# Chunk attention and two feed-forward layers on one core: another way to the transposes of q, k and the softmax weights

## The chip, the cores and the metric

The kernel runs on one core of one Trainium2 chip. The metric is the device time of one execution in microseconds; the median of the runs counts. Engines: TensorE (PE, with its weight loads as PEld), VectorE (DVE), ScalarE (ACT), GpSimd (POOL), and SyncE (SP), whose queue issues all DMAs here.

## The reference

Attention within chunks of 64 tokens, then two feed-forward layers on 4608 tokens of 512 features:

```python
scores = scale * matmul(q_c, k_c.T)              # q, k, v: (8, 8, 576, 64), chunks of 64
attn = exp(scores - max(scores))
attn = attn / (sum(attn) + 1e-09)
out = matmul(attn, v_c)                          # (8, 8, 576, 64)
x = out.transpose(0, 2, 1, 3).reshape(4608, 512)
h = x @ w_in;  g = h * sigmoid(1.702 * h);  x = g @ w_out                        # 512 -> 2048 -> 512
h = x @ w_in2; g = max(h, 0) + alpha * min(h, 0); out = g @ w_out2
```

## The kernel before, in words

Tokens are handled in 36 groups of 128 (two chunks of 64) and in blocks of 512 (four groups). Blocks 0 to 6 pass through the first layer in the plain way, one after another; each has 16 steps n (`NF`), one for each 128 of the 2048 hidden features. A step issues twelve matmuls into `psH` (`emit_h`, L599), a sigmoid-gelu and an fp32r cast of it on ACT (L609, L612), the subtraction that gives the low part on DVE (`gs`, L617), and, up to two steps later, twelve matmuls into `psY` (`emit_y`, L629). At a block's last step two y steps are issued, at its first one, at its second none. The last step of a block also splits the next block's x into high and low parts (`split_x`, L573 and L575, on ACT and DVE, once the block's last h matmuls are done), and after the last y step, in the next block's first step, four copies `ysb` (two on ACT, two on DVE, L642 and L644) are stored by four DMAs (L645). The second layer follows and is not touched by the change.

The attention of later groups is woven into these steps. `between` maps a half-slot (two for each step: one in the middle of `emit_h`, before `gs`; one after `emit_y`) to functions that are called there. A group has a base half-slot; from the fifth group in `GROUP_ORDER` on, bases are six half-slots apart (`PERIOD`), so a group's position relative to a block's start takes one of three values. Before the change a group g of the ninth and later (28 of them) goes like this:

- 24 to 20 half-slots before its base, `sort_qk` copies quarters of q and k from DRAM to a DRAM scratch tensor by eight strided DMAs (16 if the group straddles two batches); `load_sorted` (12 before) loads them sorted by two DMAs.
- `att_T` (6 before): two DVE transposes in 32x32 blocks (L402) give q and k with features on the partitions.
- The matmuls of S (`att_S_matmuls`, L449) are issued with `att_PV` of the group before, two half-slots before the base; `att_S_max` (1 before) takes the maximum and subtracts it on DVE (L460, L462); `att_X` is the exponential on ACT (L469, with an activation table load ahead of it and another ahead of the next gelu).
- `att_N` (at the base): sum, reciprocal, product on DVE (L474 to L477). `att_AT` (1 after): eight DVE transposes of 32 partitions each (L509), which put each 32x32 quadrant where it belongs. `att_PV` (4 after): 32 matmuls of 64x64 (L542), and then ACT copies to x.

Beside that, the second layer's weights are prepared every six half-slots: loads (`raw`, L242), decoding on DVE (L180 to L196), splits (`sta`, `stb`: a cast on ACT, a subtraction on POOL, L276) and stores two half-slots later (`send_due`, L253). Each engine and SP's queue take their instructions strictly in the order in which they are written.

Of the kernel before, what the change touches and what calls it, by code (L numbers as in the profile page):

```python
# [9 lines left out]
F32 = mybir.dt.float32  # L10
# [5 lines left out]
ALU = mybir.AluOpType  # L16
AX = mybir.AxisListType
# [47 lines left out]
def tile_chunk_attention_two_ffn(  # L65
# [269 lines left out]
    def load_qkv(g, names="qkv"):  # L335

        for nm in names:
            if g < GPB:
                t = {
                    "q": lambda: spare(f"wi{NF - GPB + g}", 0),  # L340
                    "k": lambda: spare(f"wi{NF - GPB + g}", 1),
                    "v": lambda: spare(f"wo{NF - 1 - g // 2}", g % 2),
                }[nm]()
            else:
                t = qkv_p.tile([P, 512], F32, tag=nm, name=nm, bufs=1 if nm == "v" else 2)
# [8 lines left out]
    def load_v(g):  # L354
        load_qkv(g, "v")

    qk_d = {}
    QK_AT = {GPB + 2: 3, GPB + 3: 9}

    def sort_qk(part, g):  # L360


        nm, src = (("q", q), ("k", k))[part // 4]
        if part % 4 == 0:
            qk_d[g, nm] = dram.tile([4, P, HP, SQ], F32, name=f"{nm}d_{g}")
        par, y = divmod(part % 4, 2)
        for off, n, b, s in spans(g * P, P):
            nc.sync.dma_start(
                out=qk_d[g, nm][part % 4, off:off + n],
                in_=src[b, par::2, s:s + n, y * SQ:(y + 1) * SQ].rearrange("h t e -> t h e"),  # L370
            )

    def load_sorted(g):
        for nm in ("q", "k"):
            t = qkv_p.tile([P, 512], F32, tag=nm, name=nm, bufs=2)
            nc.sync.dma_start(
                out=t, in_=qk_d.pop((g, nm)).rearrange("r (t b) h e -> (r t) (b h e)", b=4)
            )
            qkv[g, nm] = t

    qkT = {}

    def att_T(g):

        copies = []
        for nm in ("q", "k"):
            a = qkv.pop((g, nm))
            if g < GPB:
                t = spare(f"wo{NF - 3 - g % 2}", nm == "k").rearrange("p (h t) -> p h t", h=HP)
            else:  # L390
                t = qkt_p.tile([P, HP, P], F32, tag=nm + "T", name=nm + "T")
            if g < 2 * GPB:
                ps = psum_att("psT")
                for hp in range(HP):
                    nc.tensor.transpose(
                        ps[:, hp * P:(hp + 1) * P],
                        a[:, 2 * hp:2 * hp + 2, :].rearrange("p h d -> p (h d)"),
                        ident,
                    )
                copies.append((t.rearrange("p h t -> p (h t)"), ps))  # L400
            else:
                nc.vector.transpose(  # L402
                    t.rearrange("p h (t b) -> p b h t", b=4),
                    a.rearrange("p (b h e) -> p b h e", b=4, h=HP),
                )
            qkT[g, nm] = t
        for copy in copies:
            nc.scalar.copy(*copy)  # L408
# [31 lines left out]

    def att_S_matmuls(g):

        qt, kt = qkT.pop((g, "q")), qkT.pop((g, "k"))
        s_t[g] = s4 = both[0][:, :, HP * CH:].rearrange("p j (h t) -> p h j t", h=HP)
        for hp in range(HP):
            for c in range(2):
                for j in range(2):
                    r = slice(j * CH, (j + 1) * CH)
                    nc.tensor.matmul(  # L449
                        s4[c * CH:(c + 1) * CH, hp, j, :],  # L450
                        qt[r, hp, c * CH:(c + 1) * CH],
                        kt[r, hp, c * CH:(c + 1) * CH],
                        start=True,
                        stop=True,
                    )

    def att_S_max(g):
        s4 = s_t.pop(g)
        m = st_p.tile([P, HP, 2, 1], F32, tag="m", name="m")
        nc.vector.reduce_max(m, s4, axis=AX.X)  # L460
        e = e_p.tile([P, 2 * HP, CH], F32, tag="e", name="e")
        nc.vector.tensor_tensor(  # L462
            out=e.rearrange("p (h j) t -> p h j t", j=2), in0=s4,
            in1=m.to_broadcast([P, HP, 2, CH]), op=ALU.subtract,
        )
        e_t[g] = e

    def att_X(g):
# [1 line left out]

    def att_N(g):
        e = e_t[g]
        d = st_p.tile([P, 2 * HP, 1], F32, tag="d", name="d")
        nc.vector.reduce_sum(d, e, axis=AX.X)  # L474
        nc.vector.tensor_scalar_add(d, d, 1e-9)
        nc.vector.reciprocal(d, d)
        (nc.gpsimd if g < GPB - 1 or g in GROUP_ORDER[:GPB] else nc.vector).tensor_tensor(  # L477
            out=e, in0=e, in1=d.to_broadcast([P, 2 * HP, CH]), op=ALU.mult
        )

    def att_E(g):
        att_X(g)
        att_N(g)

    at_t = {}

    def att_AT(g):
        e = e_t.pop(g)
        if g < GPB:
            t = spare(f"wi{NF - GPB - 1 - g}", 1).rearrange("p (h t) -> p h t", h=HP)  # L490
        else:
            t = at_p.tile([P, HP, P], F32, tag="at", name="at")

        if g >= GPB:
            if g < 2 * GPB:
                ps = psum_att("psAT")
                for u in range(2 * HP):
                    for c in range(2):
                        r = slice(c * CH, (c + 1) * CH)
                        nc.tensor.matmul(  # L500
                            ps[r, u * CH:(u + 1) * CH], e[r, u, :], ident[r, r], start=True, stop=True
                        )
                nc.scalar.copy(t.rearrange("p h t -> p (h t)"), ps)
            else:
                t3 = t.rearrange("p h (j t) -> p (h j) t", j=2)
                for i in range(P // SQ):
                    for b in range(CH // SQ):
                        o = i // 2 * 2 + b
                        nc.vector.transpose(  # L509
                            t3[o * SQ:(o + 1) * SQ, :, i % 2 * SQ:(i % 2 + 1) * SQ],  # L510
                            e[i * SQ:(i + 1) * SQ, :, b * SQ:(b + 1) * SQ],
                        )
# [13 lines left out]
    def att_PV(g):  # L526
# [12 lines left out]
        for hp in range(HP):  # L539
            for c in range(2):  # L540
                for j in range(2):
                    nc.tensor.matmul(  # L542
                        ps[c][j * CH:(j + 1) * CH, hp * CH:(hp + 1) * CH],
                        vt[c * CH:(c + 1) * CH, 2 * hp + j, :],
                        at[c * CH:(c + 1) * CH, hp, j * CH:(j + 1) * CH],
                        start=True,
                        stop=True,
                    )
# [553 lines left out]
    with tc.manual_schedule():  # L1102
# [68 lines left out]
        def base(i):  # L1171
            return FIRST_BASES[i] if i < GPB else 8 * GPB + PERIOD * (i - GPB)
# [3 lines left out]
        for i, g in enumerate(GROUP_ORDER):  # L1176
            if i < GPB:
                times = ((att_T, -5), (att_X, -1), (att_N, 0), (att_AT, 3), (att_PV, 4))
            else:
                times = (  # L1180
                    (att_T, -6 if i > GPB else -8), (att_S_max, -1), (att_X, -1), (att_N, 0), (att_AT, 1), (att_PV, 4),
                )
            for fn, at in times:
                if g > GPB or fn is not att_T:
# [124 lines left out]
```

## Time and profile before

| | |
|---|---|
| median of 3 runs | 1554.39 us (1553.26 to 1555.19) |
| profiled execution, first to last instruction (span) | 1552.8 us; the profile gives no other time of its own, and the median lies 1.6 us above it |
| busy: PE, DVE, ACT, POOL | 1538.1, 1234.8, 894.1, 607.6 us |
| instructions | 25251 |
| DMA packets | 470282, of which 252688 under 512 B; 316.26 MB |

The page shows engines by busy time, the span in 40 slices, the DMA queues, the chain of work that ended last, and the costliest groups of instructions. A timeline row gives the start, the length and the engine of one or more like instructions; brackets at its end give the engine's idle time ahead of it and what ended that.

### The profile page before, as it was taken

To read this page: it belongs to the slowest core of one execution; us is meant where nothing else is said; L and a number is where in the kernel's file an instruction comes from. 1 tells how busy PE (TensorE), PEld (TensorE's weight loads), DVE (VectorE), ACT (ScalarE), POOL (GpSimd) and SP (SyncE) were. 2 spreads that over 40 slices of the span, in tenths; PEclk is the share of its full clock that TensorE was granted. 3 is DMA by queue.
4 is the path that set the end of the run, shared out by engine and by line. 5 is a ranking of instruction groups with operands and counts; after the bars stand their busy time and mean duration, and the time that the engine had idled before them with its cause. 6 is when DMAs were issued, how large, how long until landed. Compare 5 with 4: busy or idle time off the path is not lost.

```text
span 1552.8 us, 25251 instructions
## 1 busy us (share of the span) xinstructions
PE 1538.1 (99%) x9263; PEld 1293.5 (83%) x9265; DVE 1234.8 (80%) x1550; ACT 894.1 (58%) x1284; POOL 607.6 (39%) x535
## 2 busy tenths in 40 slices
PE   8999999999999999999999999999999999999998
PEld 5777888888888888888888888888888888999998
DVE  7999888888897988673898678777877788778777
ACT  6776555454554545457665656555656556556663
POOL 0003545445454454437662252225222423342330
PEclk9999999999999999999999999999999999999999
DMA  9945668768777855665335776688668866997974
GB/s 256 321 96 146 169 187 218 196 176 214 202 194 191 234 158 149 194 197 147 97 111 154 249 246 192 192 209 286 190 190 218 260 192 207 247 350 234 270 259 149
DMA packets 470282, 316.26 MB, mean 204 GB/s; under 512 B 252688, under 2 KB 401040, under 8 KB 470160
## 3 DMA queue, kind: packets, MB, share of 16 engines
q1 hardware_dynamic: 470160, 314.67, 70.8%
q8 instruction: 73, 1.20, 0.3%
q14 instruction: 49, 0.40, 0.1%
HBM read 249.57 MB, written 79.69 MB: 212 GB/s over the span
## 4 chain that ended last, share of the span: by engine, by line
PE 92%; DVE 5%; ACT 2%; issue 1%; DMA 0%; SPq 0%; ACTq 0%; DVEq 0%
PE psY L629 19%; PE psH L599 18%; PE psYa L974 15%; PE psHa L841 15%; PE psYb L974 11%; PE psHb L841 11%; PE psX L542 1%; PE psX L449 1%; DVE o L917 1%; DVE yacc L1012 0%; DVE u L191 0%; DVE g L892 0%; DVE at L509 0%; ACT neg L858 0%; ACT early L408 0%
## 5 line engine op out<-in xcount | busy, mean ns | idle before, releaser
L599 PE MATMUL psH<-xs,wi 128*128 128x512 f32 x1344 | 324.5, 391 | 2.0 <-ACT xs L145 1.0
L629 PE MATMUL psY<-gs,wo 128*128 128x512 f32 x1296 | 314.2, 392 | 0.0
L599 PEld LDWEIGHTS psH<-xs,wi 128*128 128x128 f32 x1344 | 251.2, 188 | 56.1 <-DVE wi L148 1.5
L629 PEld LDWEIGHTS psY<-gs,wo 128*128 128x128 f32 x1296 | 240.9, 188 | 51.2
L841 PE MATMUL psHa<-xop,wi2t 128*128 128x512 f32 (+1 forms) x852 | 190.7, 372 | 0.0
L922 POOL TENSOR_TENSOR tsum<-g,tsum 128x1024 f32<-128x1024 f32 (+1 forms) x46 | 121.6, 2644 | 163.0 <-DVE o L917 124.7
L974 PE MATMUL psYa<-o,w 128*128 128x512 f32 (+1 forms) x816 | 184.3, 374 | 0.9 <-DVE o L917 0.8
L841 PEld LDWEIGHTS psHa<-xop,wi2t 128*128 128x128 f32 x852 | 156.6, 188 | 23.2
L974 PEld LDWEIGHTS psYa<-o,w 128*128 128x128 f32 x816 | 149.8, 188 | 24.5 <-DVE o L917 1.8
L922 POOL TENSOR_TENSOR tsum<-g,g 128x1024 f32<-128x1024 f32 (+1 forms) x23 | 51.5, 2239 | 294.7 <-DVE g L864 276.9
L609 ACT ACTIVATE g<-psH 128x512 f32<-128x512 f32 x108 | 64.4, 597 | 174.5 <-PE psH L599 174.1
L856 ACT ACTIVATE neg<-g 128x1024 f32<-128x1024 f32 (+1 forms) x80 | 78.1, 976 | 128.9 <-DVE g L892 128.3
L841 PE MATMUL psHb<-xop,wi2t 128*128 128x512 f32 (+1 forms) x660 | 146.7, 371 | 0.0
L974 PE MATMUL psYb<-o,w 128*128 128x512 f32 (+1 forms) x636 | 142.4, 372 | 0.4 <-DVE o L917 0.4
L841 PEld LDWEIGHTS psHb<-xop,wi2t 128*128 128x128 f32 x660 | 121.1, 188 | 17.2
L974 PEld LDWEIGHTS psYb<-o,w 128*128 128x128 f32 x636 | 116.6, 188 | 17.7 <-DVE o L917 0.7
L617 DVE TENSOR_TENSOR gs<-g,gs 128x512 fp32r<-128x512 f32 x108 | 90.2, 835 | 28.7 <-ACT gs L612 27.7
L917 DVE TENSOR_TENSOR o<-tsum,o 128x1024 fp32r<-128x1024 f32 (+1 forms) x52 | 61.1, 1175 | 61.8 <-ACT o L912 61.5
L864 DVE SCALAR_TENSOR_TENSOR g<-g,neg 128x1024 f32<-128x1024 f32 (+1 forms) x80 | 102.0, 1275 | 9.2 <-ACT neg L858 9.2
L1012 DVE TENSOR_TENSOR yacc<-psYb,yacc 128x1024 f32<-128x1024 f32 (+1 forms) x64 | 72.2, 1128 | 44.6 <-PE psYb L974 44.6
L858 ACT ACTIVATE neg<-neg,minus_alpha 128x512 f32<-128x512 f32 (+1 forms) x160 | 100.2, 674 | 2.6
L509 DVE STREAM_TRANSPOSE at<-e 32x256 f32<-32x256 f32 x224 | 97.4, 435 | 3.1
(177 smaller groups left out, 2659.3 us busy)
## 6 DMA issues: line engine op xcount, KB each, us to landing
w<-wo SPq DMA_DIRECT2D x140, 512.0 KB, 3.8
wi2t<-wi SPq DMA_DIRECT2D x210, 256.0 KB, 3.7
w<-wi SPq DMA_DIRECT2D x70, 256.0 KB, 3.6
raw<-in_moe_w_in_dram SPq DMA_DIRECT2D x16, 512.0 KB, 6.5
raw<-in_moe_w_out_dram SPq DMA_DIRECT2D x16, 512.0 KB, 6.5
raw<-in_moe_w_in_dram SPq DMA_DIRECT2D x32, 256.0 KB, 4.5
raw<-in_moe_w_out_dram SPq DMA_DIRECT2D x32, 256.0 KB, 4.1
v<-in_v_dram SPq DMA_DIRECT2D x28, 256.0 KB, 4.4
```

The costliest lines, as they stand in the source:

```text
L509: nc.vector.transpose(t3[o * SQ:(o + 1) * SQ, :, i % 2 * SQ:(i % 2 + 1) * SQ], e[i * SQ:(i + 1) * SQ, :, b * SQ:(b + 1) * SQ],)
L599: nc.tensor.matmul(ps, w[:, a, c], xs[:, b, c], start=(i == 0), stop=(i == 3 * KT - 1))
L617: nc.vector.tensor_tensor(out=gs[:, 1], in0=g, in1=gs[:, 0].bitcast(F32), op=ALU.subtract)
L629: nc.tensor.matmul(y_t[j][t], w[:, a, t * P:(t + 1) * P], gs[:, b], start=(f == 0 and a + b == 0), stop=(f == NF - 1 and b == 1),)
L841: nc.tensor.matmul(ps, w[:, c, a], x[b][:, c], start=(k == 0 and i in (1, 2, 5)), stop=(k == 5 and i in (2, 3, 4)), skip_group_check=True,)
L856: nc.scalar.activation(out=neg, in_=src, func=AF.Relu, scale=-1.0)
L858: nc.scalar.activation(out=neg[:, jj], in_=neg[:, jj], func=AF.Copy, scale=minus_alpha[:, f + jj:f + jj + 1])
L864: nc.vector.scalar_tensor_tensor(out=g, in0=g, scalar=0.0, in1=neg, op0=ALU.max, op1=ALU.add)
L917: nc.vector.tensor_tensor(out=lo, in0=wide(homes[nm], n), in1=hi.bitcast(F32), op=ALU.subtract)
L922: eng.tensor_tensor(out=wide(homes[out], n), in0=wide(homes[x], n), in1=wide(homes[y], n), op=ALU.subtract,)
L974: nc.tensor.matmul(ps[:, d, :n], w[:, jj, d, a], x[b][:, jj], start=(k == 0 and i in (1, 5, 2)), stop=(k == 5 and i in (3, 2, 4)), skip_gr ...
L1012: nc.vector.tensor_tensor(out=out_acc, in0=ps[:, :, :n], in1=acc, op=ALU.add)
```

## The change

For the 28 groups from the ninth on, q and k are loaded unsorted (`load_nat`: two tokens, 512 B, a run), straight from the inputs into SBUF. `qk_T` transposes them at full width on DVE, and ACT copies the 128x1024 result to a second tile `D`; `qk_swap` then moves the quadrants that came out in the wrong place from the first tile to `D`, by four SBUF-to-SBUF DMAs. The softmax weights, laid out in halves of 32, are transposed twice at full width (into `pt` and into `at`), and `at_swap` moves the misplaced quadrants from `pt` to `at` by four DMAs. q, k and the intermediate tiles share two buffers ("nat"). The times relative to the base change as the last hunk shows.

```diff
-    def sort_qk(part, g):
...
-    def load_sorted(g):
...
+    def load_nat(g):
+        nat_t[g] = qkv_p.tile([P, 2, 512], F32, tag="nat", name="nat", bufs=2)
+        for i, src in enumerate((q, k)):
+            for off, n, b, s in spans(g * P, P):
+                for par in range(2):
+                    p0 = par * CH + off // 2
+                    nc.sync.dma_start(
+                        out=nat_t[g][p0:p0 + n // 2, i].rearrange("p (h x) -> p h x", h=HP),
+                        in_=src[b, par::2, s:s + n, :].rearrange("h (s i) d -> s h (i d)", i=2),
+                    )
+
+    def swap_quads(dst, src):
+        for r in range(0, P, CH):
+            for a in range(2):
+                nc.sync.dma_start(
+                    out=dst[r + (1 - a) * SQ:r + (2 - a) * SQ, a], in_=src[r + a * SQ:r + (a + 1) * SQ, 1 - a]
+                )
+
+    def qk_T(g):
+        nat = nat_t.pop(g)
+        t = qkv_p.tile([P, 2, 2, HP, CH], F32, tag="nat", name="qkt", bufs=2)
+        for i in range(2):
+            nc.vector.transpose(
+                t[:, :, i].rearrange("p y h (s i) -> p y h i s", i=2),
+                nat[:, i].rearrange("p (h i y e) -> p y h i e", h=HP, i=2, y=2),
+            )
+        d = d_t[g] = qkt_p.tile([P, 2, 2, HP, CH], F32, tag="D", name="D")
+        nc.scalar.copy(
+            d.rearrange("p y i h t -> p (y i h t)"), t.rearrange("p y i h t -> p (y i h t)")
+        )
+        qk_s[g] = t
+
+    def qk_swap(g):
+        flat = "p y i h t -> p y (i h t)"
+        swap_quads(d_t[g].rearrange(flat), qk_s.pop(g).rearrange(flat))
...
     def att_S_max(g):
...
+            s4 = s4.rearrange("p h j t -> p j h t")
+            m = st_p.tile([P, 2, HP, 1, 1], F32, tag="m", name="m")
+            nc.vector.reduce_max(m[:, :, :, 0], s4, axis=AX.X)
+            e = e_p.tile([P, 2, 2 * HP, SQ], F32, tag="e", name="e")
+            nc.vector.tensor_tensor(
+                out=e.rearrange("p b (j h) t -> p j h b t", j=2),
+                in0=s4.rearrange("p j h (b t) -> p j h b t", b=2),
+                in1=m.to_broadcast([P, 2, HP, 2, SQ]), op=ALU.subtract,
+            )
...
+    def at_swap(g):
+        flat = "p b u t -> p b (u t)"
+        swap_quads(at_t[g].rearrange(flat), pt_t.pop(g).rearrange(flat))
...
-                t3 = t.rearrange("p h (j t) -> p (h j) t", j=2)
-                for i in range(P // SQ):
-                    for b in range(CH // SQ):
-                        o = i // 2 * 2 + b
-                        nc.vector.transpose(
-                            t3[o * SQ:(o + 1) * SQ, :, i % 2 * SQ:(i % 2 + 1) * SQ],
-                            e[i * SQ:(i + 1) * SQ, :, b * SQ:(b + 1) * SQ],
-                        )
+                pt = pt_t[g] = qkv_p.tile([P, 2, 2 * HP, SQ], F32, tag="nat", name="pt", bufs=2)
+                flat = "p b u t -> p (b u t)"
+                for o in (pt, t):
+                    nc.vector.transpose(o.rearrange(flat), e.rearrange(flat))
...
-                        at[c * CH:(c + 1) * CH, hp, j * CH:(j + 1) * CH],
+                        at[c * CH:(c + 1) * CH, :, j * HP + hp] if g >= 2 * GPB
+                        else at[c * CH:(c + 1) * CH, hp, j * CH:(j + 1) * CH],
...
-                    (att_T, -6 if i > GPB else -8), (att_S_max, -1), (att_X, -1), (att_N, 0), (att_AT, 1), (att_PV, 4),
+                    (load_nat, -10), (qk_T, -7), (qk_swap, -6), (att_S_max, -1), (att_X, -1), (att_N, 0),
+                    (att_AT, 1), (at_swap, 2), (att_PV, 4),
...
-            if g >= 2 * GPB:
-                for part in range(8):
-                    when = base(i) - 24 + part * 6 // 8
-                    between.setdefault(when, []).append((partial(sort_qk, part), g))
-                between.setdefault(base(i) - 12, []).append((load_sorted, g))
```

Since `qk_T` of a group lies 7 half-slots before its base, it is issued in the half-slot of the `att_S_max` and `att_X` of the group before, after them.

## Rows read from the trace of the kernel before

**Rows 1.** The page, busy time: engine, us (share of the span) xinstructions.
```profile
PE 1538.1 (99%) x9263; PEld 1293.5 (83%) x9265; DVE 1234.8 (80%) x1550; ACT 894.1 (58%) x1284; POOL 607.6 (39%) x535
```
**Rows 2.** Waits of PE, whole span: us in total, times, longest.
```profile
PE psX L542 <- DVE at L509: 0.5, 2, 0.3
```
**Rows 3.** Timeline, a regular group: start, us, engine, line, operation.
```profile
370.91 0.69 PE L542 MATMUL psX<-at,v 64*64 64x64 f32 x32
...
374.69 0.69 DVE L462 TENSOR_TENSOR e<-psX,m 128x512 f32<-128x512 f32 x1
...
375.42 0.63 ACT L469 ACTIVATE e<-e 128x512 f32<-128x512 f32 x1 [1.31 <-DVE e L462]
...
376.07 1.28 ACT L609 ACT_TABLE_LOAD   x1
...
377.77 0.60 ACT L609 ACTIVATE g<-psH 128x512 f32<-128x512 f32 x1 [0.42 <-PE psH L599]
377.86 1.10 DVE L402 STREAM_TRANSPOSE qT<-q 128x512 f32<-128x512 f32 x1
378.40 0.62 ACT L612 CAST gs<-g 128x512 fp32r<-128x512 f32 x1
...
379.57 1.01 POOL L276 TENSOR_TENSOR u<-u,sta 128x384 fp32r<-128x384 f32 x1 [3.81 <-issue]
...
381.05 3.60 DVE L509 STREAM_TRANSPOSE at<-e 32x256 f32<-32x256 f32 x8
...
382.45 0.55 SPq L253 DMA_DIRECT2D wi<-sta  x1
...
383.09 0.43 SPq L253 DMA_DIRECT2D wi<-u  x1
...
384.69 0.69 DVE L617 TENSOR_TENSOR gs<-g,gs 128x512 fp32r<-128x512 f32 x1
...
388.55 0.64 PE L542 MATMUL psX<-at,v 64*64 64x64 f32 x28
```
**Rows 4.** Groups of DVE by form: count | busy us, mean ns | idle before.
```profile
L509 DVE STREAM_TRANSPOSE at<-e 32x256 f32<-32x256 f32 x224 | 97.4, 435 | 3.1
...
L1026 DVE STREAM_TRANSPOSE x_b<-yacc 128x512 f32<-128x512 f32 x12 | 7.8, 682 | 0.0
```
**Rows 5.** Groups by form, 250 to 650 us: a 128x1024 operation of ACT.
```profile
L733 ACT CAST xop<-xtop 128x1024 fp32r<-128x1024 f32 x1 | 1.0, 1037 | 0.0
```
**Rows 6.** DMA view, 414 to 426 us: GB/s by slice; issues, KB each, us to landing.
```profile
GB/s 199 342 399 344 280 201 194 297 323 313 382 260 120 31 3 0 0 164 416 294 0 0 0 253 382 396 430 410 382 364 31 105 169 250 327 327 225 167 90 171
...
x<-ysb SPq DMA_DIRECT2D x4, 256.0 KB, 2.2
...
wi<-sta SPq DMA_DIRECT2D x1, 192.0 KB, 3.1
```
**Rows 7.** Timeline, a group with `att_N` in the first step of block 4.
```profile
413.51 0.69 DVE L462 TENSOR_TENSOR e<-psX,m 128x512 f32<-128x512 f32 x1
...
418.43 3.06 SPq L645 DMA_DIRECT2D x<-ysb  x4
...
419.48 1.28 DVE L642 COPY ysb<-psY 128x512 f32<-128x512 f32 x2
...
424.33 0.62 PE L542 MATMUL psX<-at,v 64*64 64x64 f32 x26 [0.17 <-DVE at L509]
```
**Rows 8.** Timeline, a group with the split of x between maximum and sums (block 5).
```profile
506.59 1.09 DVE L402 STREAM_TRANSPOSE qT<-q 128x512 f32<-128x512 f32 x1
...
515.23 0.69 PE L542 MATMUL psX<-at,v 64*64 64x64 f32 x32
```
**Rows 9.** Timeline, the group with `att_N` in the first step of block 1.
```profile
130.70 0.69 DVE L462 TENSOR_TENSOR e<-psX,m 128x512 f32<-128x512 f32 x1
...
131.97 0.60 ACT L217 COPY u<-raw 128x512 f32<-128x512 f32 x1
...
141.27 0.62 PE L542 MATMUL psX<-at,v 64*64 64x64 f32 x26 [0.29 <-DVE at L509]
```

More of the change, by code (lines that the diff above doesn't have):

```diff
@@ L343, in load_qkv @@
                 }[nm]()
-            else:
-                t = qkv_p.tile([P, 512], F32, tag=nm, name=nm, bufs=1 if nm == "v" else 2)
+            elif nm == "v":
+                t = qkv_p.tile([P, 512], F32, tag="v", name="v")
+            else:
+                if nm == "q":
+                    pair = qkv_p.tile([P, 2, 512], F32, tag="nat", name="qk", bufs=2)
+                t = pair[:, "qk".index(nm)]
             t = t.rearrange("p (h d) -> p h d", h=H)
@@ L355, in load_v @@
         load_qkv(g, "v")
-    qk_d = {}
     QK_AT = {GPB + 2: 3, GPB + 3: 9}
-    def sort_qk(part, g):
[L363 to L370, printed above, removed]
-            )
@@ L373, in load_sorted @@
-    def load_sorted(g):
[L374 to L377, printed above, removed]
-            )
-            qkv[g, nm] = t
+    nat_t = {}
+    def load_nat(g):
[8 more added lines that the diff above has]
+                    )
@@ new lines, in swap_quads @@
+    def swap_quads(dst, src):
[4 more added lines that the diff above has]
+                )
+    qk_s, d_t = {}, {}
+    def qk_T(g):
[5 more added lines that the diff above has]
+                nat[:, i].rearrange("p (h i y e) -> p y h i e", h=HP, i=2, y=2),
+            )
+        d = d_t[g] = qkt_p.tile([P, 2, 2, HP, CH], F32, tag="D", name="D")
[3 more added lines that the diff above has]
+        qk_s[g] = t
@@ L390, in att_T @@
             else:
[L391 to L401, printed above, removed]
-                nc.vector.transpose(
-                    t.rearrange("p h (t b) -> p b h t", b=4),
-                    a.rearrange("p (b h e) -> p b h e", b=4, h=HP),
+                if nm == "q":
+                    d = qkt_p.tile([P, 2, HP, P], F32, tag="D", name="DT")
+                t = d[:, "qk".index(nm)]
+            ps = psum_att("psT")
+            for hp in range(HP):
+                nc.tensor.transpose(
+                    ps[:, hp * P:(hp + 1) * P],
+                    a[:, 2 * hp:2 * hp + 2, :].rearrange("p h d -> p (h d)"),
+                    ident,
                 )
+            copies.append((t.rearrange("p h t -> p (h t)"), ps))
             qkT[g, nm] = t
@@ L441, in att_S_matmuls @@
     def att_S_matmuls(g):
-        qt, kt = qkT.pop((g, "q")), qkT.pop((g, "k"))
+        if g < 2 * GPB:
+            qt, kt = (qkT.pop((g, nm)).rearrange("p h (c t) -> p c h t", c=2) for nm in "qk")
+        else:
+            d = d_t.pop(g)
+            qt, kt = d[:, :, 0], d[:, :, 1]
         s_t[g] = s4 = both[0][:, :, HP * CH:].rearrange("p j (h t) -> p h j t", h=HP)
@@ L450, in att_S_matmuls @@
                         s4[c * CH:(c + 1) * CH, hp, j, :],
-                        qt[r, hp, c * CH:(c + 1) * CH],
-                        kt[r, hp, c * CH:(c + 1) * CH],
+                        qt[r, c, hp],
+                        kt[r, c, hp],
                         start=True,
@@ L458, in att_S_max @@
         s4 = s_t.pop(g)
[L459 to L465, printed above, removed]
+        if g < 2 * GPB:
+            m = st_p.tile([P, HP, 2, 1], F32, tag="m", name="m")
+            nc.vector.reduce_max(m, s4, axis=AX.X)
+            e = e_p.tile([P, 2 * HP, CH], F32, tag="e", name="e")
+            nc.vector.tensor_tensor(
+                out=e.rearrange("p (h j) t -> p h j t", j=2), in0=s4,
+                in1=m.to_broadcast([P, HP, 2, CH]), op=ALU.subtract,
+            )
+        else:
+            s4 = s4.rearrange("p h j t -> p j h t")
+            m = st_p.tile([P, 2, HP, 1, 1], F32, tag="m", name="m")
+            nc.vector.reduce_max(m[:, :, :, 0], s4, axis=AX.X)
+            e = e_p.tile([P, 2, 2 * HP, SQ], F32, tag="e", name="e")
+            nc.vector.tensor_tensor(
+                out=e.rearrange("p b (j h) t -> p j h b t", j=2),
+                in0=s4.rearrange("p j h (b t) -> p j h b t", b=2),
+                in1=m.to_broadcast([P, 2, HP, 2, SQ]), op=ALU.subtract,
+            )
         e_t[g] = e
@@ L472, in att_N @@
         e = e_t[g]
+        split_rows = g >= 2 * GPB
+        if split_rows:
+            e = e.rearrange("p b u t -> p u b t")
         d = st_p.tile([P, 2 * HP, 1], F32, tag="d", name="d")
-        nc.vector.reduce_sum(d, e, axis=AX.X)
+        nc.vector.reduce_sum(d, e, axis=AX.XY if split_rows else AX.X)
         nc.vector.tensor_scalar_add(d, d, 1e-9)
         nc.vector.reciprocal(d, d)
+        if split_rows:
+            d = d.rearrange("p u (o n) -> p u o n", o=1)
         (nc.gpsimd if g < GPB - 1 or g in GROUP_ORDER[:GPB] else nc.vector).tensor_tensor(
-            out=e, in0=e, in1=d.to_broadcast([P, 2 * HP, CH]), op=ALU.mult
+            out=e, in0=e, in1=d.to_broadcast(list(e.shape)), op=ALU.mult
         )
@@ L483, in att_E @@
         att_N(g)
-    at_t = {}
+    at_t, pt_t = {}, {}
+    def at_swap(g):
+        flat = "p b u t -> p b (u t)"
+        swap_quads(at_t[g].rearrange(flat), pt_t.pop(g).rearrange(flat))
     def att_AT(g):
@@ L490, in att_AT @@
             t = spare(f"wi{NF - GPB - 1 - g}", 1).rearrange("p (h t) -> p h t", h=HP)
+        elif g >= 2 * GPB:
+            t = at_p.tile([P, 2, 2 * HP, SQ], F32, tag="at", name="at")
         else:
@@ L504, in att_AT @@
             else:
-                t3 = t.rearrange("p h (j t) -> p (h j) t", j=2)
-                for i in range(P // SQ):
-                    for b in range(CH // SQ):
-                        o = i // 2 * 2 + b
-                        nc.vector.transpose(
-                            t3[o * SQ:(o + 1) * SQ, :, i % 2 * SQ:(i % 2 + 1) * SQ],
-                            e[i * SQ:(i + 1) * SQ, :, b * SQ:(b + 1) * SQ],
-                        )
+                pt = pt_t[g] = qkv_p.tile([P, 2, 2 * HP, SQ], F32, tag="nat", name="pt", bufs=2)
+                flat = "p b u t -> p (b u t)"
+                for o in (pt, t):
+                    nc.vector.transpose(o.rearrange(flat), e.rearrange(flat))
         else:
```

## Prediction

> **What bounds the kernel now.** I read the page first: TensorE (PE) is busy 99% of the span [rows 1], and the chain that ended last is its matmuls one after another. So the second question is what PE still waits for. The list of PE's waits over the whole span has one entry that this change can touch: the matmuls of `att_PV` waited 0.5 us in all, twice, for the softmax weights that DVE transposes at L509 [rows 2]. The list's other entries lie in the opening or in the second layer: in the changed stretch PE runs back to back, with 17.64 us from one `att_PV` to the next [rows 3]. Two things follow. Time saved on DVE, ACT or the DMA queue is worth at most that 0.5 us, about 0.03%. And whatever makes `att_PV` (or the matmuls of S) wait longer is lost one for one, because PE has no slack later to make it up. The work is then to find, by the timeline, when the new chain in front of `att_PV` ends, in each of the positions in which a group can stand.
>
> **The change, part by part.** *VectorE.* Removed: eight quarter transposes of 0.435 us for each group, 3.48 us. Added: two full 128x512 ones, contiguous on both sides; the nearest row is the transpose of L1026, 0.68 us [rows 4], so 1.36 us (up to 1.10 each, as L402 with its scattered writes [rows 3]). The two transposes of q and k stay two, with a gentler pattern (runs of 32 in, every second element out): between 0.68 and 1.10, and I take 0.9, nearer to what is there. Together 5.7 us become 3.2 for each of 28 groups, some 70 us of VectorE time, all of it off the path of PE.
>
> *ScalarE.* Added: one 128x1024 copy a group (`D`), 1.04 us [rows 5]. It is queued right behind the exponential and waits for both q,k transposes. Queued behind it are the table load, the sigmoid-gelu of the running step, its fp32r cast, the cast for the weight store, and at a block's start two copies of `ysb`; for them wait DVE's `gs` subtraction, DVE's transposes in `att_AT` behind that, GpSimd's subtraction, and SP's stores.
>
> *SP and the DMA engines.* Removed a group: eight strided transfers to DRAM (16 where a group straddles two batches) and two loads back. Added: four loads (eight), and eight SBUF-to-SBUF transfers. The four for q and k are issued four half-slots before their matmuls and I cost them at nothing: what hides them is two thirds of the 17.64 us period. The four for the weights stand between `att_AT` and `att_PV`, where before there was nothing. They are queued on SP behind two weight stores, and at a block's first step behind the four stores of `ysb`. Their price is not in the trace. An issue of this size takes 0.43 to 0.55 us [rows 3]; I take 0.5, with 0.65 above. Landing: the four 256 KB stores of `ysb` took 2.2 us from issue, the 192 KB store of `sta` 3.1 [rows 6]. Moving 256 KB at the 400 GB/s of that stretch is 0.65 us of the 2.2, so 1.55 is the lower bound for 32 KB. I take 2.2, since these queue behind others; 3.1 is the upper bound. From the end of `att_AT` (or the stores ahead) to the last landing is then 3 x 0.5 + 2.2 = 3.7 us.
>
> The Trainium skill ("DMA: Bandwidth & Descriptors", Rules for kernel authors) speaks against such transfers: under 64 KB mostly overhead is paid, and transfers to disjoint partition ranges are said to serialize. Row and rule differ if that means one after another: the four `ysb` stores were issued within 3.06 us [rows 7] and their median landing was still 2.2 us, where in a line it would have been near 5.
>
> *TensorE.* `att_PV` reads its moving operand in two runs of 32 instead of one of 64. The trace has no such read; I take nothing. The 32 matmuls stand in 0.69 us [rows 8]; as much again in 28 groups would be 19 us, which I leave to the second rival's range.
>
> **A regular group** (22 of 28, block starts elsewhere) [rows 3]. The subtraction of the maximum ends at 375.4. The q,k transposes now come next: 377.2. Copy: 378.2. Table load 1.28: 379.5. Gelu 0.60: 380.1. Cast 0.62: 380.75. `gs` 0.69: 381.4. `att_AT` 1.36: 382.8, while today it ends at 384.65. SP: GpSimd's subtraction began 1.80 us after the gelu's start, so now at 381.3, and ends at 382.3; the two weight stores are out by 383.3; the swaps have landed at 387.0. PE comes to `att_PV` at 388.55. Spare: 1.5 us; with every upper bound (0.4 for the transposes, 0.45 for issues, 0.9 for landing) it is 0.2 too late, with every lower one 2.8 spare. No loss.
>
> **A group whose `att_N` falls into a block's first step** (two: blocks 1 and 4). Here there are fewer y matmuls between, PE already waits today, and DVE is held by the split of x until late. Block 4 [rows 7]: subtraction ends at 414.2; transposes 416.0; copy 417.05; table 418.3; gelu 418.9; cast 419.55; `gs` 420.25; the two `ysb` copies 1.28: 421.5; `att_AT` 422.9. SP has to send the `ysb` stores first; the last waits for DVE's second copy, 422.3, then the two weight stores, 423.3, then the swaps: the fourth is issued at 424.8 and lands at 427.0. Today PE goes on at 424.33. Loss: 2.7 us. Block 1 [rows 9]: 131.4; 133.2; 134.2; two more ACT copies of 0.6 ahead of the table load, 135.5; 136.8; gelu 137.4; cast 138.0; `gs` 138.7; `ysb` 140.0; `att_AT` 141.35; last swap issued at 142.85, landed at 145.05. Today PE goes on at 141.27. Loss: 3.8 us.
>
> The table load decides part of that. In the row it lasts 1.28 us, begins 0.02 us after the exponential and the engine is ready for the gelu at its end (377.35, then 0.42 of waiting for PE) [rows 3]. The Trainium skill ("ScalarE: Activation LUTs", What ACT_TABLE_LOAD costs) adds a drain of 1.38 us to each switch. The trace shows none; with it the two losses would be 9.3 us together instead of 6.5.
>
> **A group in which the split of x comes between its maximum and its sums** (two: blocks 2 and 5) [rows 8]. The maximum, the exponential and the new copy lie ahead of the split, so nothing is pushed. `att_N` ends at 506.6, `gs` 507.3, `att_AT` 508.65, swaps landed at 512.35; `att_PV` starts at 515.23. No loss. In blocks 3 and 6 two y steps lie ahead of `att_PV`, more spare than a regular group.
>
> **Sum.** 2.7 + 3.8 = 6.5 us. The profiled span of 1552.8 us becomes 1559.3. The median of the runs, 1554.39, lies 1.6 above the span, so 1560.9. Bounds: each loss is 1.3 shorter with all lower bounds (0.65 landing, 0.45 transposes, 0.2 issues) and 1.75 longer with all upper ones, so 3.9 to 10.0 us, 1558.3 to 1564.4.
>
> **Rivals.**
> 1. *The swaps are hidden everywhere.* This needs the chain at both block starts 2.7 and 3.8 us shorter than I make it, below all my lower bounds, for instance because the stores land sooner and DVE gets to the maximum earlier there. For it: DVE does lose 2.5 us of work a group. Against: at both places the maximum follows the split, which waits for PE. Time: 1552.8 - 0.5 + 1.6 = 1553.9, and with a rest of a microsecond or two still no measurable change.
> 2. *The regular groups lose too.* A spare of 1.5 us is little: a later gelu, a weight store that waits longer for GpSimd, or landings of 3.1 us with transposes of 1.10 turn it round. At 0.2 to 1.2 us in 22 groups it adds 4 to 26 us to the 6.5: 1565 to 1587, in the middle 1575.
> 3. *The swaps go one after another.* Four times 2.2 is 8.8 us from 383.3: 392.1, 3.55 us late in 22 groups, 7.8 and 8.9 at the block starts, 95 us, 1649. The `ysb` rows speak against it. This is the reading of the rule named above.
> 4. *Faster.* The other side: DVE's relief removes the wait at `att_PV`. It is one mechanism with a ceiling of 0.5 us where PE waits for L509, and could pass 0.2% only if PE waited for DVE six times as long; no row shows that.
>
> **How the numbers follow.** 0.2% is 3.1 us, about what a measurement of this kernel can tell from no change. Forecast (losses at two block starts only) 0.54; rival 1 0.20; rival 2 0.21; rival 3 0.02; rival 4 0.03. The forecast's time is 1560.9, its own range 1558.3 to 1564.4. For 8 in 10 the range takes in rival 1, which is near, and rival 2 to a little past its middle: 1553.6 to 1577. Left out are the upper part of rival 2 (0.09), rivals 3 and 4, and a little of the lower edge. Slower by over 0.2%: 0.54 + 0.21 + 0.02, less 0.01 for the forecast's lower end, 0.76; same: 0.21; faster: 0.03.
>
> **What would show it.** In the profile after: L509's successor as two transposes of about 0.7 us each; an ACT copy of about 1 us between exponential and table load; PE's list of waits with `att_PV` behind a DMA, in two places, near 141 and 424 us, by 2.5 to 4 us each, and the period of 17.64 us between two `att_PV` elsewhere unchanged; DMA packets under 512 B down. The prediction is wrong if PE waits for the swaps in most groups (period above 17.64), if it waits nowhere, or if the matmuls of `att_PV` themselves take longer than 0.69 us.

## The result, and the profile after

The changed kernel takes **1577.09 us** (median of 4 runs, 1576.32 to 1580.73) against 1554.79 us before (4 runs, 1553.26 to 1556.66): a ratio of **1.0148, 95% interval 1.0133 to 1.0162**. The forecast, 1560.9 us, had the sign; the size is more than three times the forecast one, just above the range. The profiled run has a span of 1574.2 us, 21.4 more than before, and its own time is 1576.32 us.

The page after (busy time, as [rows 1]; the packets), PE's waits over the whole span (as [rows 2]), and the groups and DMA issues that are new:

```profile
PE 1547.6 (98%) x9265; PEld 1301.2 (83%) x9265; DVE 1153.0 (73%) x1382; ACT 923.0 (59%) x1312; POOL 601.7 (38%) x535
...
DMA packets 384972, 312.62 MB, mean 199 GB/s; under 512 B 138704, under 2 KB 319312, under 8 KB 384848
```
```profile
PE psX L587 <- DMA at<-pt: 8.7, 6, 2.7
PE psX L587 <- DVE u L196: 4.1, 1, 4.1
PE psH L645 <- ACT wi L145: 2.6, 1, 2.6
```
```profile
L394 DVE STREAM_TRANSPOSE qkt<-nat 128x512 f32<-128x512 f32 x56 | 36.7, 689 | 2.9 <-DMA nat<-in_k_dram 2.8
...
L557 DVE STREAM_TRANSPOSE pt<-e 128x512 f32<-128x512 f32 x28 | 19.7, 703 | 0.0
L557 DVE STREAM_TRANSPOSE at<-e 128x512 f32<-128x512 f32 x28 | 18.7, 669 | 0.0
...
L399 ACT COPY D<-qkt 128x1024 f32<-128x1024 f32 x28 | 29.4, 1052 | 24.2 <-DVE qkt L394 24.2
```
```profile
D<-qkt SPq DMA_DIRECT2D x112, 64.0 KB, 2.0
...
at<-pt SPq DMA_DIRECT2D x112, 32.0 KB, 2.3
```

The change did what it says: DVE has 82 us less work, ACT 29 more, and the small packets have nearly halved. The price is in PE's waits: `att_PV` now waits 12.8 us for the exchanged weights, in seven waits. The second row is counted with them although it names `u`: `att_PV` reads nothing of `u`. Its wait ended at 442.47 us; `u` at L196 ended just before, at 442.38, and the four exchanges issued from 438.97 landed between 442.0 and 442.7 (the rows are below). The third wait is not at the exchange at all.

To place all 21.4 us I noted, in both timelines, the start of the first y matmul behind each `att_PV` and S, and took the difference, the offset. It stays constant, within 0.04 us, from one group to the next, except here:

| place | first y matmul, before | after | offset grows by |
|---|---|---|---|
| first 36 us (kernel start) | 35.65 | 37.03 | 1.38 |
| opening, the wait for `wi` L145 | 117.61 | 123.86 | 4.87 |
| the step behind it | 124.24 | 129.44 | -1.05 |
| group at the start of block 1 | 142.35 | 149.77 | 2.22 |
| group behind the start of block 2 | 248.19 | 258.48 | 2.87 |
| group behind the start of block 3, and the next | 336.68 | 350.62 | 3.64 + 0.53 |
| group at the start of block 4, and the next | 425.40 | 444.77 | 4.90 + 1.25 |
| group behind the start of block 5 | 531.25 | 553.28 | 1.41 |
| group behind the start of block 6 | 618.98 | 641.67 | 0.62 |

That is 6.25 in the opening, of which 1.05 comes back in the next step (PE waited 0.72 us there in the kernel before and no longer does), 17.44 at six places of the layer, 0.05 in small change, and the rest of the program gives 1.3 back: 21.4. The expectations below count the 1.05 against block 1 and so say 16 us for the six places. A regular group loses nothing, and its period is still 17.64 us. Timeline after, a regular group (answers to [rows 3]):

```profile
385.38 0.69 PE L587 MATMUL psX<-at,v 64*64 64x64 f32 x32
...
395.13 0.67 DVE L557 STREAM_TRANSPOSE at<-e 128x512 f32<-128x512 f32 x1
...
396.31 2.49 SPq L382 DMA_DIRECT2D at<-pt  x4
...
403.02 0.69 PE L587 MATMUL psX<-at,v 64*64 64x64 f32 x32
```

The weights are ready at 395.80, the four exchanges are out at 398.80, and with the median landing of 2.3 us the fourth (issued at about 398.2) is there at 400.5: 2.5 us before `att_PV`, which also takes its usual 0.69 us. (Its own landing took 1.9 us, which makes the spare 2.9.)

Timeline after, the group behind the start of block 3:

```profile
330.68 0.69 PE L587 MATMUL psX<-at,v 64*64 64x64 f32 x32
...
338.24 1.05 ACT L399 COPY D<-qkt 128x1024 f32<-128x1024 f32 x1 [0.58 <-DVE qkt L394]
...
339.30 1.28 ACT L655 ACT_TABLE_LOAD   x1
...
340.60 0.60 ACT L655 ACTIVATE g<-psH 128x512 f32<-128x512 f32 x1
...
342.08 1.31 SPq L242 DMA_DIRECT2D raw<-in_moe_w_in_dram  x2
...
342.79 2.88 PE L645 MATMUL psH<-xs,wi 128*128 128x512 f32 x12
343.12 0.67 DVE L557 STREAM_TRANSPOSE at<-e 128x512 f32<-128x512 f32 x1
...
343.49 0.55 SPq L253 DMA_DIRECT2D wi<-sta  x1
...
344.13 0.43 SPq L253 DMA_DIRECT2D wi<-u  x1
...
344.65 2.48 SPq L382 DMA_DIRECT2D at<-pt  x4
...
348.42 1.31 PE L587 MATMUL psX<-at,v 64*64 64x64 f32 x30 [2.74 <-DMA at<-pt]
...
350.62 1.54 PE L675 MATMUL psY<-gs,wo 128*128 128x512 f32 x3
```

Here PE has done all other work by 345.6, only 14.9 us after the `att_PV` before it: in this interval lies the step at a block's start that has no y matmuls to issue, so one y step of 2.72 us is missing. From the end of `att_AT` at 343.79 the weights need 0.86 until SP has sent the stores, 2.48 for four issues, and PE goes on 1.3 later. Then PE also runs slow: the three y matmuls last 0.51 us each, not 0.25.

`att_AT` itself is late here: it ends 13.1 us after the `att_PV` before it, in the regular group 10.4, and so only 1.9 us before PE has nothing else to do (7.2 in the regular group). In the kernel before, this place had no spare either; its transposes ended at 335.55, 0.25 us after PE had begun `att_PV`:

```profile
331.95 3.60 DVE L509 STREAM_TRANSPOSE at<-e 32x256 f32<-32x256 f32 x8
...
335.30 0.93 PE L542 MATMUL psX<-at,v 64*64 64x64 f32 x30
```

Timelines after, the same place of block 2 (SP), block 4 (SP, DVE, PE) and the opening (ACT, PE), one below the other:

```profile
247.88 3.04 SPq L382 DMA_DIRECT2D D<-qkt  x4
250.96 1.31 SPq L242 DMA_DIRECT2D raw<-in_moe_w_in_dram  x2
...
253.54 2.48 SPq L382 DMA_DIRECT2D at<-pt  x4
```
```profile
434.94 2.19 SPq L691 DMA_DIRECT2D x<-ysb  x4
...
437.19 0.99 SPq L253 DMA_DIRECT2D wi<-sta  x1
438.27 0.61 SPq L253 DMA_DIRECT2D wi<-u  x1
438.97 2.52 SPq L382 DMA_DIRECT2D at<-pt  x4
```
```profile
436.01 0.67 DVE L557 STREAM_TRANSPOSE at<-e 128x512 f32<-128x512 f32 x1
...
441.56 0.82 DVE L196 SCALAR_TENSOR_TENSOR u<-raw,u 128x512 int32<-128x512 int32 x1
```
```profile
442.47 1.41 PE L587 MATMUL psX<-at,v 64*64 64x64 f32 x30 [4.10 <-DVE u L196]
```
```profile
114.87 1.04 ACT L399 COPY D<-qkt 128x1024 f32<-128x1024 f32 x1 [5.08 <-DVE qkt L394]
115.82 0.61 ACT L145 CAST wo<-u 128x512 fp32r<-128x512 f32 x1
116.34 0.61 ACT L145 CAST wi<-u 128x512 fp32r<-128x512 f32 x1
```
```profile
117.01 5.49 PE L645 MATMUL psH<-xs,wi 128*128 128x512 f32 x12 [2.58 <-ACT wi L145]
```

In block 2 `att_AT` is done at 250.57 and SP comes to the exchange at 253.54: it is still busy with the exchange of q and k of the next group, the two loads of weights queued behind it, and two stores. In block 4 `att_AT` is done at 436.68 and SP is 2.29 late, behind the stores of `ysb` and of the weights. In the opening the new copy waits 5.08 us for DVE, and two weight casts that PE needs stand behind it in ACT's order.

Windows after, PE's clock at four of these waits (busy time of PE, PEld, DVE, ACT, POOL, then granted clock, DMA share, GB/s):

```profile
117.00:119.00 2.00, 1.99 (x5) 1.61 (x6) 2.00 (x6) 2.00 (x4) 0.00 (x0) 0.50 0.42 98
```
```profile
442.00:444.00 2.00, 1.53 (x46) 1.48 (x49) 1.24 (x2) 0.00 (x0) 1.89 (x3) 0.50 0.36 97
```
```profile
350.00:352.00 2.00, 2.00 (x27) 1.66 (x21) 1.58 (x3) 1.23 (x3) 1.43 (x3) 0.52 0.89 248
```
```profile
148.00:150.00 2.00, 1.56 (x65) 1.49 (x66) 1.87 (x3) 0.41 (x2) 1.92 (x3) 1.00 0.39 106
```

After waits of 2.58, 2.74 (block 3) and 4.10 us PE ran for some microseconds at the lower of its two levels, 1.2 GHz; after 2.51 us (block 1) it did not.

### The profile page after: what moved, and what is told of

It is laid out like the page before. It is cut to its first block, busy times and chain, and to the rows that moved or that the text cites. A ratio compares the mean times of both kernels' runs of the same rounds, so it can differ in the third digit from the quotient of the medians.

```text
span 1574.2 us, 25368 instructions
## 1 busy us (share of the span) xinstructions
PE 1547.6 (98%) x9265; PEld 1301.2 (83%) x9265; DVE 1153.0 (73%) x1382; ACT 923.0 (59%) x1312; POOL 601.7 (38%) x535
## 4 chain that ended last, share of the span: by engine, by line
PE 88%; DVE 6%; ACT 2%; SPq 2%; DMA 1%; issue 1%; DVEq 0%; ACTq 0%
PE psY L675 17%; PE psH L645 15%; PE psYa L1020 15%; PE psHa L887 15%; PE psYb L1020 11%; PE psHb L887 11%; PE psX L587 1%; SPq L382 1%; PE psX L476 1%; DMA at<-pt 1%; DVE u L191 1%; DVE u L180 0%; PE warm L1163 0%; DVE gs L663 0%; DVE qkt L394 0%
## 5 line engine op out<-in xcount | busy, mean ns | idle before, releaser
L663 DVE TENSOR_TENSOR gs<-g,gs 128x512 fp32r<-128x512 f32 x108 | 84.3, 781 | 132.6 <-ACT gs L658 132.6
L1058 DVE TENSOR_TENSOR yacc<-psYa,yacc 128x1024 f32<-128x1024 f32 (+1 forms) x75 | 84.5, 1126 | 19.0 <-PE psYa L1020 18.6
```

Of the source, the lines that this page charges most:

```text
L663: nc.vector.tensor_tensor(out=gs[:, 1], in0=g, in1=gs[:, 0].bitcast(F32), op=ALU.subtract)
L1058: nc.vector.tensor_tensor(out=out_acc, in0=ps[:, :, :n], in1=acc, op=ALU.add)
```

## The experiments

Theory: the exchange of the weights is the loss in the layer, because it stands in SP's order behind other DMAs and between `att_AT` and an `att_PV` that comes a y step early. Rivals: the ScalarE copy, which makes everything behind it late; the exchange of q and k, which holds SP; the new layout's reads in `att_PV` itself. Each run is compared with the kernel before on the same chip (1554.15 to 1554.29 us).

**No exchange of the weights.**
```diff
-                    (att_AT, 1), (at_swap, 2), (att_PV, 4),
+                    (att_AT, 1), (att_PV, 4),
```


> Leaves out the exchange of the softmax weights' quadrants (at_swap); everything else of the change stays. Theory A (the exchange of the weights sits on PE's path in the six groups next to a block start, 16 us in all, and the opening loses 6 us by itself): PE's waits for at<-pt go, those six losses go, the opening's stays: about 1561 us. Rival B (the new ScalarE copy delays the gelu and with it att_AT, and that is what PE waits for): att_PV still waits in most of the six places, now for DVE, and at least half of the 16 us stays: 1569 or more.

Measured: 1554.71 us, ratio 1.0006 [0.9996, 1.0015]. No wait is left at any of the six places. Timeline of block 3:
```profile
334.41 0.67 DVE L557 STREAM_TRANSPOSE at<-e 128x512 f32<-128x512 f32 x1
...
336.89 0.69 PE L587 MATMUL psX<-at,v 64*64 64x64 f32 x32
```
So without the weights' exchange the copy on ACT, the new transposes, the loads and the q,k exchange together cost PE nothing in the layer, nor do the split reads of `att_PV`; the offset even shrinks by 1.6 us there, at blocks 1, 3 and 4 above all. The opening's wait of 2.6 us stayed, but the offset grew there by 2.1 instead of 4.9 us.

**No exchange of q and k.**
```diff
-                    (load_nat, -10), (qk_T, -7), (qk_swap, -6), (att_S_max, -1), (att_X, -1), (att_N, 0),
+                    (load_nat, -10), (qk_T, -7), (att_S_max, -1), (att_X, -1), (att_N, 0),
```


> Leaves out the exchange of the quadrants of q and k (qk_swap); everything else of the change stays. Theory D (part of A: the four q,k exchanges, 0.62 to 0.87 us each on SP's queue, are what makes the exchange of the weights late): the weights' exchange is issued up to 2.5 us sooner in blocks 2, 3, 5 and 6, the losses there shrink from 9.1 us to under 2: about 1568 us. Rival (what counts is only the weights' own issue and landing after att_AT): less than 3 us gained, 1574 or more.

Measured: 1568.6 us, 1.0092 [1.0077, 1.0107]. Block 2 loses 0.5 instead of 2.9, block 3 2.0 instead of 4.2, block 4 4.1 instead of 6.2, block 5 nothing instead of 1.4. In block 2 `att_AT` ends at 250.92, and SP comes to the exchange 0.15 us later instead of 2.97:
```profile
251.06 2.51 SPq L382 DMA_DIRECT2D at<-pt  x4
```
So the four q,k transfers, which PE never waits for, cost 8.0 us in blocks 2 to 5, part of it by the clock: they keep the weights' exchange from SP. That the whole comes out 8.5 us lower (7.2 in the profiled spans) is partly chance, for here the opening keeps 1.4 us less and block 1, where the clock now falls to 0.50, loses 1.9 us more.

**Old q,k path, new weights' path** (the q,k sort through DRAM as before; `pt` lies in one of the five buffers in which the second layer's weights are decoded, and what that costs is not separated).
```diff
-                    (load_nat, -10), (qk_T, -7), (qk_swap, -6), (att_S_max, -1), (att_X, -1), (att_N, 0),
-                    (att_AT, 1), (at_swap, 2), (att_PV, 4),
+                    (att_T, -6 if i > GPB else -8), (att_S_max, -1), (att_X, -1), (att_N, 0), (att_AT, 1), (at_swap, 2), (att_PV, 4),
```


> q and k as before (sorting through DRAM, no ScalarE copy, no q,k exchange); the softmax weights as changed (two full transposes and the exchange). Theory A with D: the opening's loss is gone, the losses in blocks 2, 3, 5 and 6 shrink to about nothing, blocks 1 and 4 keep 2 to 3 us each, as their stores of ysb lie ahead on SP: about 1559 us. If the exchange alone costs the 16 us wherever it stands: about 1571.

Measured: 1579.18 us, 1.0165 [1.0148, 1.0183]. Far from what I expected: with the old sort `att_PV` waits 16.6 us in nine waits (the profile is of the slowest of the four runs, 1584.34 us). Block 3:
```profile
343.23 0.66 DVE L539 STREAM_TRANSPOSE at<-e 128x512 f32<-128x512 f32 x1
...
345.51 1.26 SPq L368 DMA_DIRECT2D qd<-in_q_dram  x2
...
348.04 2.48 SPq L507 DMA_DIRECT2D at<-pt  x4
...
350.79 0.48 PE L569 MATMUL psX<-at,v 64*64 64x64 f32 x4 [4.76 <-DMA at<-pt]
```
The sort's transfers stand in front of the exchange, beside loads and stores of weights: it is issued 4.15 us after `att_AT`'s end, against 0.86 in the full change. The opening's 4.9 us are gone, since there is no copy. The weights' exchange is dear with whatever SP has in front of it.

**New q,k path, old weights' path** (`att_S_max`, `att_X`, `att_N`, `att_AT` and `att_PV` as before).
```diff
-                    (att_AT, 1), (at_swap, 2), (att_PV, 4),
+                    (att_AT, 1), (att_PV, 4),
```


> q and k as changed (unsorted loads, ScalarE copy, exchange); the softmax weights as before (eight quarter transposes, no exchange). Theory A: no DMA between att_AT and att_PV, so only the opening loses (6 us) and blocks 1, 3 and 4 lose under 1 us each where the 3.5 us of transposes now start late behind the copy: about 1562 us. Rival B (the ScalarE copy is the cost): the waits stay, PE waits for DVE in the six places: 1570 or more.

Measured: 1559.96 us, 1.0037 [1.0024, 1.0050]. The offset grows by 1.3 at the start, 2.1 in the opening (the `wi` wait of 2.6 us), 3.1 around block 1, where `att_PV` waits 1.8 us for the quarter transposes that the copy now delays, 0.2 each in blocks 3 and 4, and nowhere else.

**The same with the first group's q and k earlier.**
```diff
-                    (load_nat, -10), (qk_T, -7), (qk_swap, -6), (att_S_max, -1), (att_X, -1), (att_N, 0),
+                    (load_nat, -10 if i > GPB else -16), (qk_T, -7 if i > GPB else -10), (qk_swap, -6 if i > GPB else -9), (att_S_max, -1), (att_X, -1), (att_N, 0),
```


> The softmax weights as before (eight quarter transposes, no exchange), q and k as changed, and for the first of the 28 groups loads, transposes and exchange of q and k three to six half-slots earlier, so that ScalarE's copy is past before the weight casts that PE waits for. The opening's loss of 2 us goes; what is left is 2 to 3 us in block 1: about 1557 us, within 0.2% of before. If the early copy disturbs the opening elsewhere: 1560 or more.

Measured: 1559.5 us, 1.0034 [1.0022, 1.0046]. The `wi` wait fell from 2.6 to 1.2 us in two pieces, the total only by 0.5, which is no more than its scatter. Neither version beats the kernel before.

**The exchange ahead of the weight stores.**
```diff
-                    (att_AT, 1), (at_swap, 2), (att_PV, 4),
+                    (att_AT, 1), (at_swap, 1), (att_PV, 4),
```


> at_swap one half-slot earlier, directly behind att_AT, so that on SP's queue it comes ahead of the two weight stores. Queue theory (SP issues one DMA after another, about 0.6 us each, and the weights' exchange stands behind them): it is issued up to 1 us sooner where the queue is late (blocks 2, 3, 5 and 6), the losses there shrink by about 1 us each, blocks 1 and 4 by up to 1: about 1572 us. Rival (the landing alone is too long): no change, 1577.

Measured: 1574.91 us, 1.0137 [1.0123, 1.0151]: `att_PV` waits 11.1 us in ten places. Passing two stores (about 1 us of SP) shortens the waits by 1.7 us. The layer gains nothing by it: its six places lose 18.9 us instead of 17.4, for blocks 3 and 4 lose 2.9 less, but blocks 1 and 2 lose 4.5 more. That the total is 2.2 us lower (1.2 in the profiled spans) comes from the start and the opening, which lose 2.9 us less, before the first exchange is issued.

**The exchange a half-slot later.**
```diff
-                    (att_AT, 1), (at_swap, 2), (att_PV, 4),
+                    (att_AT, 1), (at_swap, 3), (att_PV, 4),
```


> at_swap one half-slot later, so that on SP's queue the loads of q and k (2.6 us, 4.6 where a group straddles two batches) stand ahead of it. Theory A: a regular group has about 2.6 us to spare (fourth issue at 398.2 and landing 2.2 us later against 403.0 in the profile of the changed kernel), so most regular groups lose nothing or a few tenths; the six places lose 2.6 us more each: about 1594 us. If regular groups stood as close to the edge as the prediction's upper bounds (spare near 0), 22 times 2.6 us more: about 1650 us.

Measured: 1599.49 us, 1.0291 [1.0275, 1.0306]. 2.7 us of delay is about what a regular group has to spare: most regular groups now lose 0 to 0.5 us (one 1.1), the groups that end at the start of blocks 2 and 5 lose 4.5, and the six places lose up to 9.5.

**The exchange on ACT's queue.**
```diff
-        swap_quads(at_t[g].rearrange(flat), pt_t.pop(g).rearrange(flat))
+        swap_quads(at_t[g].rearrange(flat), pt_t.pop(g).rearrange(flat), nc.scalar)
```


> The four DMAs of the weights' exchange are issued from ScalarE's queue instead of SP's, at the same place in the program. Queue theory: in blocks 2 and 5, where att_AT ended 3 us ahead of the issue, the loss goes; in blocks 3 and 6 it shrinks by under 1 us, since att_AT ends there less than 2 us before att_PV is due and four issues and a landing take over 4 us; blocks 1 and 4 gain 1 to 3 us: about 1569 us. Rival (landing and issues after att_AT decide, not the queue): less than 3 us gained, 1574 or more. ScalarE's own work could lose by the issues (some 2.5 us a group): above 1577.

Measured: 1597.11 us, 1.0277 [1.0263, 1.0291]; 25.0 us of waits in 23 places, since the issues now stand behind the gelu and the cast of the running step. Block 3 is the reading that matters, for there the queue was free:
```profile
351.77 0.67 DVE L557 STREAM_TRANSPOSE at<-e 128x512 f32<-128x512 f32 x1
352.47 2.48 ACTq L382 DMA_DIRECT2D at<-pt  x4
...
356.85 0.33 PE L587 MATMUL psX<-at,v 64*64 64x64 f32 x4 [2.52 <-DMA at<-pt]
```
Issued 0.03 us after `att_AT`'s end, the weights are still 2.5 us late. With no queue in front, four issues and a landing (4.4 us) alone are more than this place has, since `att_AT` ends only 1.9 us before PE is free. So in block 3 the queue is not the main cause of the wait; the late end of `att_AT` in a short interval is.

**Two of the four transfers** (the other misplaced quadrants stay where they are).
```diff
-        swap_quads(at_t[g].rearrange(flat), pt_t.pop(g).rearrange(flat))
+        swap_quads(at_t[g].rearrange(flat), pt_t.pop(g).rearrange(flat), (0,))
```


> Leaves out two of the four DMAs of the softmax weights' exchange (the ones into the second half of the columns). Theory A with the price of an issue (each DMA holds SP's queue 0.62 us, the last landing follows 2 us after the last issue): the last landing comes 1.2 us sooner in each of the six places; where the whole loss was under 1.5 us (blocks 5 and 6, part of 1) it goes, in blocks 2, 3 and 4 it shrinks by 1.2 us and more where the half clock stays away: about 1569 us. Rival (one landing alone is what makes it late): under 3 us gained, 1574 or more.

Measured: 1570.26 us (1566.23 to 1573.74), 1.0111 [1.0094, 1.0128]. In block 3:
```profile
338.16 0.67 DVE L557 STREAM_TRANSPOSE at<-e 128x512 f32<-128x512 f32 x1
...
339.72 1.21 SPq L382 DMA_DIRECT2D at<-pt  x2
...
342.59 0.73 PE L587 MATMUL psX<-at,v 64*64 64x64 f32 x30 [1.87 <-DMA at<-pt]
```
Two issues fewer save 1.27 us of SP, and the wait falls by 0.87. The runs spread by 7.5 us, so only the direction is taken from the total.

**The copy on GpSimd** (so that ACT's gelu comes earlier).
```diff
-        nc.scalar.copy(
+        nc.gpsimd.tensor_copy(
```


> The 128x1024 copy of q and k runs on GpSimd instead of ScalarE. Rival B (the copy in front of table load and gelu holds up att_AT): gelu and att_AT come 1.6 us sooner, the six losses shrink by 1 to 1.5 us each, and the opening's wait for the weight cast goes: about 1565 us. Queue theory: att_AT comes sooner but q and k are exchanged later, GpSimd's copy being 2 us and queued behind other work, and the weights' exchange stands behind that on SP: no gain in the six places or a loss; only the opening gains 2 us: 1575 to 1585.

Measured: 1579.97 us, 1.0167 [1.0154, 1.0181]. The copy takes 1.05 us there too, not the 2 expected. The `wi` L145 wait is gone, a wait of 1.3 us for the DVE half of `wi` (L148) takes its place, and the offset grows by 1.9 in the opening instead of 4.9; so most of the opening's loss is the copy's. The six places lose more than with ACT. For the layer the run decides less than it seems: in block 3 `att_AT` does end 3.2 us before PE is free instead of 1.9, so the copy had held it up by 1.3, but SP comes to the exchange 2.2 us after it instead of 0.9, as q and k are exchanged later. The gain and the loss cancel there.

## Why the prediction fell short

*Right: the mechanism and the unit prices.* The weights' exchange is the loss in the layer (taking it out brings back 1554.7 us), at block starts and not in regular groups. The transposes took 0.67 to 0.70 us (0.68 taken) and 0.69 for q and k (0.9 taken), the copy 1.05 (1.04), a landing 2.3 (2.2). An issue took 0.62, near my upper 0.65 and not the 0.5: 0.4 us on four. The table load has no drain: 339.30 + 1.28 = 340.58, and the gelu begins at 340.60; the figure of the Trainium skill ("ScalarE: Activation LUTs", What ACT_TABLE_LOAD costs) that I set against it does not show here. Nor do the four transfers go one after another: in block 3 the fourth, issued at about 346.5, landed 2.1 us later, 4.0 us after the first was issued and not 8.8. Rival 3, the reading of the Trainium skill's rule on partition ranges ("DMA: Bandwidth & Descriptors", Rules for kernel authors), is out.

*Blocks 1 and 4: 6.5 forecast, 8.4 measured.* That the sums are near is luck: block 1 lost 2.22 where I had 3.8, block 4 6.15 where I had 2.7. In block 1 `att_AT` ended 1.9 us sooner than my estimate moved by the offset (144.63 against 141.35 + 5.20). In block 4 it ended 0.7 sooner (436.68 against 422.9 + 14.47), but the `ysb` stores were out 0.4 later and the two weight stores held SP 1.8 us instead of 1.0, so the exchange was issued 1.2 later than estimated, and the clock at half added 2.5.

*The step that failed*: "A regular group (22 of 28, block starts elsewhere)", with "In blocks 3 and 6 two y steps lie ahead of `att_PV`, more spare than a regular group". For blocks 2, 3, 5 and 6 I looked at the group that ends at the block's start, which indeed loses nothing. The next group has the step without y matmuls between its S and its `att_PV`: 14.9 us instead of 17.64. My own spare of 1.5 us less 2.72 would have given a loss of 1.2 in each of four groups. Measured: 2.87, 4.17, 1.41 and 0.62, together 9.1 us. The real spare of the regular group shown is 2.5 to 2.9 us, so the missing y step alone would be about covered, and what goes beyond has other sources. In blocks 2 and 5 `att_AT` ends 4.0 and 4.2 us before PE is free, and SP comes to the exchange 3.0 and 1.6 us after it (0.5 in the regular group). In block 3 `att_AT` itself comes only 1.9 us ahead of PE, SP adds 0.9, and the clock 1.6. In block 6 `att_AT` ends 3.5 us ahead and SP is not late; there the chain is just too long.

*"I cost them at nothing"*, of the q,k exchanges, is the second miss. True of PE's wait for q and k; but their 2.5 to 3.0 us on SP push back the loads and stores behind them, in block 2 past the end of `att_AT`, and the weights queue behind those. The run without them puts that at 8.0 us in blocks 2 to 5.

*The opening, 6.25 us, had no term.* I put the copy into ACT's order of a regular group, not into that of the first new group, where it waits 5.08 us for DVE ahead of PE's weight casts. The wait of 2.58 us and the half clock after it make 4.87, and 1.05 of it comes back. The 1.38 at the very start is not of the change as far as the runs show: in kernels with the same instructions there it came out between 0 and 1.4 us.

*The clock.* I had no term for it. In block 4 `att_PV` and S took 2.30 us (442.47 to 444.77), in a regular group 1.10, and what follows lost 1.25 more: 2.5 in all. In block 3 it is 1.1 and 0.53: 1.6. In the opening the stretch from the wait's end to the y matmuls took 6.85 us (117.01 to 123.86), before 4.29: 2.6.

*The ceiling of 0.5 us* for DVE's relief was too low, though nothing hangs on it. In the kernel before `att_PV` and S took 1.70, 1.38 and 1.57 us in the table's groups at blocks 1, 3 and 4 instead of 1.10, and the list of waits shows only part of that; without the weights' exchange these 1.4 us came back.

Rival 1 (hidden everywhere) and rival 4 (faster) fell with the measured time; rival 2 (regular groups) with the unchanged period. That the measured time lies next to the range's upper end is luck: rival 2 had put that end there, and other causes filled it.

**Open.** When the clock falls: the same wait of 2.6 us in the opening cost 2.1, 3.5 and 4.9 us in three kernels (2.1, 2.4 and 3.8 one step later), and I did not find what decides. The 1.3 us that come back at the end match two waits of PE in the second layer, 0.8 and 0.4 us for `o` (L917), which the kernel before has and the changed one has not; why they go is not shown. They and the 1.6 us of relief are why the partial kernels do not add up simply: without the weights' exchange the opening's 2.1 us is given back (1554.71 us, no loss), while the new q,k path with the old weights' path keeps both waits and loses 5.7 us. Why `att_AT` ends 2.7 us later behind its `att_PV` in block 3 than in a regular group is not shown; with the copy on GpSimd it still ends 1.7 later.

## What to carry to other kernels

A new chain between two steps of a hand-made order has to be tried against the shortest distance between them, found by listing the distance in every group, not in one regular group and at the places that look special. A DMA that nobody waits for still costs if its issue stands ahead of one that somebody waits for: count the issues on the queue at that moment, at their measured 0.62 us. When the engine that sets the time is already busy for 99%, relieving another by 82 us is worth next to nothing (here 1.6 us in the layer, and no shorter time), while a new link in front of it can cost far more.

## What the runs showed of the hardware

An SBUF-to-SBUF transfer of 32 to 64 KB mostly took 0.62 us of the issuing queue, on SP's and on ACT's alike (2.48 us for four, up to 3.04 in block 2). From issue to landing it took 2.0 to 2.3 us at the median on SP's queue, 3.0 for those issued on ACT's. A 32x32-block transpose of 128x512 takes 0.67 to 0.70 us, also where it writes every second element (0.69), against 1.10 in [rows 3], and the same amount in eight quarters 3.48. A stalled TensorE can cost more than the stall where the granted clock came back at 0.50: 2.5 us on top of a wait of 4.10, 1.6 on top of 2.74.
